# Column sums of the weights' squares: GpSimd's all-reduce over the partitions in the place of a TensorE product with ones

## The chip, the core and the metric

The kernel runs on one core of one Trainium2 chip. The metric is the device time of one execution in microseconds (us). Five engines matter here: TensorE (PE, with its weight loads listed as PEld), VectorE (DVE), ScalarE (ACT), GpSimd (POOL), and SyncE (SP), whose queue issues nearly all DMAs. Each engine runs its own list of instructions strictly in order; engines meet only at semaphores.

## What is computed

Three layers follow each other: an attention with normalised q and k, then two gated or rectified matrix layers. Cut to what matters:

```python
q_n, k_n = rmsnorm(q, g_q), rmsnorm(k, g_k)          # 4 batches, 12 heads, 448 x 64
scores = 1 / np.sqrt(64) * np.matmul(q_n, k_n.transpose(0, 1, 3, 2))
attn = softmax(scores)
x = np.matmul(attn, v)                               # -> 1792 tokens x 768
x = ((x @ w_a) * (x @ w_b)) @ w_out                  # 768 -> 1536 -> 768
h = x @ w_in                                         # 768 -> 2048
g = np.maximum(h, 0.0) + alpha * np.minimum(h, 0.0)
out = g @ w2_out                                     # 2048 -> 768
```

The inputs and weights reach the kernel as 64-bit floats.

## The kernel before

The matrix layers run as stages `a`, `y`, `h`, `o`, once for each of the 4 batches (`a0 y0 h0 o0 a1 ...`). A stage is cut into units: one unit is the weights of one 128-column block (or of a part of its rows), and 12 or 18 products of 128 x 128 by 128 x 448 on TensorE. A number is held as a sum of two 16-bit floats, so each block costs three products. The list `stream` holds the units of all stages in order: 24 units for `a`, 12 for `y`, 16 for `h`, 24 for `o`, then the same again for each batch.

The first time a unit's weights are used, four steps prepare them, each a fixed number of units ahead of the unit that TensorE works on (`STEPS`): `w_load` (10 ahead) reads the raw 64-bit weights, `w_convert` (8 ahead) makes 32-bit floats of them on ScalarE and VectorE and has ScalarE sum their squares along each partition (L659, into `ss`), `w_scale` (6 ahead) sums these over the 128 partitions and derives a power of two from the total, and `w_split` (3 ahead) splits the weights into two 16-bit halves with that scale (ScalarE L706, VectorE L707) and writes them to a scratch in HBM. Later batches only read the scratch. So all of this belongs to the 76 units of batch 0. Units share a scale in groups: two columns of two units in `a` and `h`, two parts of one column in `y`, four parts in `o`. That makes 12 + 6 + 8 + 6 = 32 sums over the partitions.

Such a sum is `total` (L125 to L135): a product of the squares with a matrix of ones on TensorE (tile `tot` from `ss` and `ones`; as the operands are 32-bit, the chip runs it as two passes), and for `y` and `o` a short VectorE sum over the parts (`tots`, L131). `power` (L110 to L121) then takes three short VectorE instructions: `pw` (L115), `sc` (L118), `inv_*` (L121). `total` also serves three other sums (of v, of the products a*b, of alpha), which stay as they are.

Attention is a second stream of work. It is emitted between the units (`RATE` says how many attention steps fall on a unit), and shares ScalarE (L435 exponential, L480 probabilities), VectorE (L418 maximum, L481 probabilities) and TensorE with the weight preparation. At the end of stage `o`, four small GpSimd instructions build the output scale `cum` (L893 to L896), and one more updates `icg` (L692).

The program's order on each engine isn't the order of the source: a scheduler places each instruction where it expects it to be ready, except those marked to be kept in program order.

Of the kernel before, what the change touches and what calls it, by code (L numbers as in the profile page):

```python
# [7 lines left out]

F32 = mybir.dt.float32
# [6 lines left out]
AX = mybir.AxisListType  # L16
# [3 lines left out]
def attention_gated_mlps_kernel(  # L20
# [15 lines left out]
    nc = tc.nc  # L36
# [21 lines left out]
    sm_p = ctx.enter_context(tc.tile_pool(name="sm", bufs=4))  # L58
# [48 lines left out]
    def mm(o, a, b, first, last):  # L107
        nc.tensor.matmul(out=o, lhsT=a, rhs=b, start=first, stop=last)  # L108

    def power(total, s, i):  # L110


        n = total.shape[1]
        h = sm_p.tile([128, 4], I32, tag="pw", name="pw")[:, 0:n]
        nc.vector.tensor_scalar(  # L115
            h, total.bitcast(I32), 1, 0x7F800000, op0=ALU.logical_shift_right, op1=ALU.bitwise_and
        )
        nc.vector.tensor_scalar(  # L118
            s.bitcast(I32), h, -1.0, float(205 << 23), op0=ALU.mult, op1=ALU.add
        )  # L120
        nc.vector.tensor_scalar(i.bitcast(I32), h, 1.0, float(49 << 23), op0=ALU.mult, op1=ALU.add)  # L121

    def total(cols, n, groups=1):

        ps = ps_x.tile([128, 512], F32, tag="x", name="tot")  # L125
        p = cols.shape[0]
        mm(ps[:, 0:n], ones[:p], cols, True, True)
        if n == groups:
            return ps[:, 0:n]
        t = sm_p.tile([128, 4], F32, tag="tot", name="tots")[:, 0:groups]  # L130
        nc.vector.reduce_sum(  # L131
            out=t, in_=ps[:, 0:n].rearrange("p (g k) -> p g k", g=groups), axis=AX.X
        )
        return t
# [476 lines left out]
    for st in stages:  # L611
        n, parts, _ = CHAINS[st[0]]
# [3 lines left out]
    def size(kind):  # L616
        return CHAINS[kind][2] * 128
# [17 lines left out]
    def w_convert(u):  # L635
        if u not in raws:
            return
        kind, n, part = stream[u]
        raw = raws.pop(u)
        pair = raw.bitcast(I32).rearrange("p (n t) -> p n t", t=2)  # L640
        lo, hi = pair[:, :, 0], pair[:, :, 1]
        t = wf_p.tile([128, 768], F32, tag="wf", name="wf")[:, 0:size(kind)]
        ti = t.bitcast(I32)

        nc.scalar.activation(  # L645
            out=t, in_=hi.bitcast(F32), func=AF.Prelu, scale=2.0 ** -112, alpha=-(2.0 ** 32)
        )
        i = nc.vector.tensor_scalar(ti, ti, 3, None, op0=ALU.logical_shift_left)
        if u == 0:
            tc.keep_in_program_order(i)  # L650
        nc.vector.scalar_tensor_tensor(  # L651
            out=ti, in0=lo, scalar=29, in1=ti, op0=ALU.logical_shift_right, op1=ALU.bitwise_or
        )
        wf[u] = t
        _, parts, _ = CHAINS[kind]
        j = (n * parts + part) % (parts * GROUP[kind])
        if j == 0:
            sums[0] = sm_p.tile([128, 4], F32, tag="ss", name="ss")
        nc.scalar.activation(  # L659
            out=junk(768, size(kind)), in_=t, func=AF.Square, accum_out=sums[0][:, j:j + 1]  # L660
        )
        if j == parts * GROUP[kind] - 1:
            squares[u] = sums[0][:, 0:j + 1]

    sums, squares = [None], {}

    def w_scale(u):

        if u not in squares:
            return  # L670
        kind, n, part = stream[u]
        _, parts, _ = CHAINS[kind]
        chains = GROUP[kind]
        us = range(u - parts * chains + 1, u + 1)
        sc = sm_p.tile([128, 2], F32, tag="sc", name="sc")[:, 0:chains]
        iv = inv[kind][:, n - chains + 1:n + 1]
        power(total(squares.pop(u), len(us), chains), sc, iv)
        for x in us:
            scales[x] = sc[:, (x - us[0]) // parts:(x - us[0]) // parts + 1]
        if (kind, n) == ("h", KF2 - 1):  # L680
            h_scales()

    def h_scales():

        mx = sm_p.tile([128, 1], F32, tag="mh", name="mh")
        ci = sm_p.tile([128, 1], F32, tag="mh", name="ci")
        nc.vector.tensor_reduce(out=mx, in_=inv["h"], axis=AX.X, op=ALU.max)
        nc.vector.tensor_scalar(
            ci.bitcast(I32), mx.bitcast(I32), -1.0, float(254 << 23), op0=ALU.mult, op1=ALU.add
        )  # L690
        nc.vector.tensor_scalar(cgf, inv["h"], ci, cg, op0=ALU.mult, op1=ALU.mult)
        nc.gpsimd.tensor_tensor(icg, icg, mx, op=ALU.mult)  # L692
        state["cgf"] = True
# [3 lines left out]
    def junk(width, n):  # L697
        return one_p.tile([128, width], BF16, tag="junk", name="junk")[:, 0:n]
# [13 lines left out]


    STEPS = [(w_load, 10), (w_convert, 8), (w_scale, 6), (w_split, 3)]
    AGAIN = [(w_load, 4)]
    cur = [0]
# [202 lines left out]
    if True:  # L919
# [37 lines left out]
        for i, st in enumerate(stages):  # L957
# [4 lines left out]
            n, parts, _ = CHAINS[s]  # L962
# [38 lines left out]
```

## Time and profile before

| what | value |
|---|---|
| three runs | 1245.96, 1240.85, 1245.94 us; median 1245.94 us |
| span of the profiled execution | 1240.7 us (its own time isn't given apart from the span; the nearest run is 1240.85 us) |
| PE busy | 1169.5 us (94%) |
| ACT busy | 740.8 us (60%) |
| DVE busy | 679.8 us (55%) |
| POOL busy | 9.2 us (1%) |
| sums over partitions for the scale | 32, all between 58.7 and 425.0 us |

The shares are averages over two very different stretches: up to about 430 us all engines prepare weights and run attention together; from about 560 us on TensorE's products follow one another. A busy share must be read from the stretch that the change touches.

### The profile page before, as it was taken

The numbers are of one execution on the slowest core, as the hardware profiler recorded it, in microseconds if no ns is written. First come the engines' busy times: TensorE is split into PE (matmuls) and PEld (weight loads), VectorE is DVE, ScalarE is ACT, GpSimd is POOL, SyncE is SP. The second block draws the span as 40 slices with busy tenths as digits, with TensorE's granted clock in tenths as the row PEclk, the third lists the DMA queues.
The fourth block names the chain that finished last, engine by engine and source line by source line (L and its number), as shares of the span: only waits on it lengthen the run. The fifth ranks groups of instructions, "written<-read, shape, count | busy, mean of one in ns | idle before, by whom it ended". The sixth has DMA issues, their size and how long they took to land.

```text
span 1240.7 us, 18165 instructions
## 1 busy us (share of the span) xinstructions
PE 1169.5 (94%) x6574; PEld 598.9 (48%) x6574; DVE 679.8 (55%) x1455; ACT 740.8 (60%) x1504; POOL 9.2 (1%) x32
## 2 busy tenths in 40 slices
PE   6897998889999799989999999999999999999998
PEld 3553554444444444434455454545555555555554
DVE  7988998979999766677651466332111440102400
ACT  6998999989999966677642465543311441213311
POOL 1000000000000000000000000000000000000000
PEclk9997999897999999999999999999999999999999
DMA  6546999999999999987953737876333333344343
GB/s 185 172 139 184 287 323 306 297 277 306 302 269 300 268 258 243 228 189 183 213 160 115 177 117 164 187 190 164 102 115 115 115 115 110 106 143 131 98 126 90
DMA packets 311242, 234.67 MB, mean 189 GB/s; under 512 B 175440, under 2 KB 284496, under 8 KB 311152
## 3 DMA queue, kind: packets, MB, share of 16 engines
q1 hardware_dynamic: 311040, 233.43, 71.2%
q8 instruction: 52, 0.85, 0.3%
q0 software_dynamic: 112, 0.07, 0.1%
q14 instruction: 38, 0.31, 0.1%
HBM read 155.79 MB, written 32.24 MB: 152 GB/s over the span
## 4 chain that ended last, share of the span: by engine, by line
PE 53%; ACT 1%; DMA 1%; DVE 0%; issue 0%; SPq 0%; ACTq 0%
PE p L108 48%; PE s L108 2%; PE x L108 2%; DMA pT<-p 1%; PE p L884 1%; ACT t L877 0%; ACT pf L435 0%; PE norm L108 0%; ACT p L480 0%; DVE nm L418 0%; SPq L487 0%; DVE p L481 0%; ACT x L531 0%; PE tot L108 0%; DVE v L387 0%
## 5 line engine op out<-in xcount | busy, mean ns | idle before, releaser
L108 PEld LDWEIGHTS <-w 128*128 128x128 f16 x4896 | 475.9, 99 | 473.3 <-issue 45.3
L108 PE MATMUL p<-x,w 128*128 128x448 f16 x1728 | 335.9, 353 | 2.8 <-ACT t L780 2.0
L108 PE MATMUL p<-g,w 128*128 128x448 f16 x1152 | 230.0, 356 | 5.8 <-ACT w L706 2.5
L108 PE MATMUL p<-y,w 128*128 128x448 f16 x1152 | 223.3, 355 | 0.0
L108 PE MATMUL p<-ab,w 128*128 128x448 f16 x864 | 169.6, 356 | 1.7 <-ACT ab L761 1.6
L418 DVE TENSOR_REDUCE nm<-s 128x2 f32<-128x896 f32 x84 | 91.0, 1085 | 38.0 <-PE s L108 37.6
L480 ACT ACTIVATE p<-pf,ri 128x448 f16<-128x448 f32 x126 | 81.8, 663 | 35.3 <-DMA pT<-p 27.6
L108 PE MATMUL s<-kT,qT 128*64 128x448 f16 (+1 forms) x336 | 89.2, 433 | 14.1 <-ACT pf L435 10.3
L481 DVE SCALAR_TENSOR_TENSOR p<-pf,ri,p 128x448 f16<-128x448 f32 x126 | 84.4, 681 | 32.9 <-ACT p L480 32.7
L435 ACT ACTIVATE pf<-s,nm,esc 128x448 f32<-128x448 f32 x126 | 90.0, 718 | 1.3
L859 DVE SCALAR_TENSOR_TENSOR t<-t,al,p 128x448 f32<-128x448 f32 x55 | 37.3, 678 | 95.0 <-ACT t L858 95.0
L783 DVE SCALAR_TENSOR_TENSOR ab<-p,inv_a,t 128x448 f32<-128x448 f32 x48 | 32.6, 678 | 95.5 <-PE p L108 95.4
L707 DVE SCALAR_TENSOR_TENSOR w<-wf,sc,w 128x768 f16<-128x768 f32 (+1 forms) x76 | 70.0, 928 | 5.6 <-ACT w L706 5.3
L877 ACT ACTIVATE t<-p,inv_o 128x448 f32<-128x448 f32 x24 | 25.5, 1063 | 77.3 <-PE p L108 77.3
L645 ACT ACTIVATE wf<-raw 128x768 f32<-128x768 f32 (+1 forms) x76 | 63.1, 831 | 13.0 <-DMA raw<-in_moe_w_in_dram 5.4
L786 ACT ACTIVATE junk<-ab 128x448 bf16<-128x448 f32 x48 | 27.4, 571 | 68.1 <-DVE ab L783 68.0
L651 DVE SCALAR_TENSOR_TENSOR wf<-raw,wf 128x768 int32<-128x768 int32 (+1 forms) x76 | 66.0, 869 | 0.4
L706 ACT ACTIVATE w<-wf,sc 128x768 f16<-128x768 f32 (+1 forms) x76 | 65.0, 863 | 0.7 <-issue 0.7
L659 ACT ACTIVATE junk<-wf 128x768 bf16<-128x768 f32 (+1 forms) x76 | 58.9, 775 | 4.1 <-DVE sc L118 1.2
L858 ACT ACTIVATE t<-p 128x448 f32<-128x448 f32 x55 | 29.8, 541 | 46.8 <-PE p L108 46.4
L844 ACT ACTIVATE g<-t,cgf 128x448 f16<-128x448 f32 x55 | 36.7, 668 | 34.6 <-DVE t L859 34.6
L845 DVE SCALAR_TENSOR_TENSOR g<-t,cgf,g 128x448 f16<-128x448 f32 x55 | 37.5, 682 | 29.5 <-ACT g L844 29.5
(139 smaller groups left out, 1029.1 us busy)
## 6 DMA issues: line engine op xcount, KB each, us to landing
w<-sc_a SPq DMA_DIRECT2D x72, 384.0 KB, 3.1
w<-sc_h SPq DMA_DIRECT2D x48, 384.0 KB, 3.0
w<-sc_o SPq DMA_DIRECT2D x72, 256.0 KB, 3.1
w<-sc_y SPq DMA_DIRECT2D x36, 384.0 KB, 3.1
raw<-in_moe_w_in_dram SPq DMA_DIRECT2D x16, 768.0 KB, 7.3
raw<-in_moe_w_out_dram SPq DMA_DIRECT2D x24, 512.0 KB, 5.5
raw<-in_moe_w_a_dram SPq DMA_DIRECT2D x12, 768.0 KB, 7.0
raw<-in_moe_w_b_dram SPq DMA_DIRECT2D x12, 768.0 KB, 6.5
```

The source lines that it names most:

```text
L108: nc.tensor.matmul(out=o, lhsT=a, rhs=b, start=first, stop=last)
L418: nc.vector.tensor_reduce(out=nm, in_=ps[:, :, 0:S], axis=AX.X, op=ALU.max, negate=True)
L435: nc.scalar.activation(out=pf, in_=ps[:, j, 0:S], func=AF.Exp, bias=nm[:, j:j + 1], scale=scale[j], accum_out=su[:, j:j + 1],)
L480: nc.scalar.activation(out=t[:, 0, :, 0:KP], in_=pf, func=AF.Copy, scale=r)
L481: nc.vector.scalar_tensor_tensor(out=t[:, 1, :, 0:KP], in0=pf, scalar=r, in1=t[:, 0, :, 0:KP], op0=ALU.mult, op1=ALU.subtract,)
L645: nc.scalar.activation(out=t, in_=hi.bitcast(F32), func=AF.Prelu, scale=2.0 ** -112, alpha=-(2.0 ** 32))
L651: nc.vector.scalar_tensor_tensor(out=ti, in0=lo, scalar=29, in1=ti, op0=ALU.logical_shift_right, op1=ALU.bitwise_or)
L659: nc.scalar.activation(out=junk(768, size(kind)), in_=t, func=AF.Square, accum_out=sums[0][:, j:j + 1])
L706: nc.scalar.activation(out=w[:, 0], in_=t, func=AF.Copy, scale=s)
L707: nc.vector.scalar_tensor_tensor(out=w[:, 1], in0=t, scalar=s, in1=w[:, 0], op0=ALU.mult, op1=ALU.subtract)
L845: nc.vector.scalar_tensor_tensor(out=x[:, 1], in0=t, scalar=cgf[:, f:f + 1], in1=x[:, 0], op0=ALU.mult, op1=ALU.subtract,)
L859: nc.vector.scalar_tensor_tensor(out=t, in0=t, scalar=al[:, f:f + 1], in1=ps, op0=ALU.mult, op1=ALU.add)
```

## The change

The sum over the partitions moves from `w_scale` to `w_convert`. As soon as the squares of a group's last unit are there, GpSimd's `partition_all_reduce` adds them over the 128 partitions, and every partition gets the total (`tw`). That is emitted 8 units ahead, `w_scale` stays 6 units ahead and passes `tw` to `power`; for `y` and `o` a VectorE sum over the parts stands in between as before.

```diff
+from concourse.bass_isa import ReduceOp
...
         if j == parts * GROUP[kind] - 1:
-            squares[u] = sums[0][:, 0:j + 1]
+            squares[u] = t = sm_p.tile([128, 4], F32, tag="tw", name="tw")[:, 0:j + 1]
+            nc.gpsimd.partition_all_reduce(t, sums[0][:, 0:j + 1], 128, ReduceOp.add)
...
-        power(total(squares.pop(u), len(us), chains), sc, iv)
+        t = squares.pop(u)
+        if parts > 1:
+            one = sm_p.tile([128, 1], F32, tag="tot", name="tots")
+            nc.vector.reduce_sum(out=one, in_=t, axis=AX.X)
+            t = one
+        power(t, sc, iv)
```

The built programs show how the orders move. On TensorE, in stage `a0`, the fourth sum stood between the products of two units. Before:

```order
L108 MATMUL p<-x_5_1462,w_1205 128x448
L108 MATMUL tot<-ss,ones 128x2 [waits PE_49]
L108 LDWEIGHTS w_1317
L108 MATMUL p<-x_0_559,w_1317 128x448
L108 LDWEIGHTS w_1317
```

With the change the products follow one another (lines are up to 7 higher behind the new code):

```order
L109 MATMUL p<-x_5_1464,w_1207 128x448
L109 LDWEIGHTS w_1319
L109 MATMUL p<-x_0_559,w_1319 128x448
```

On VectorE, the power step of the tenth sum (units 18 and 19 of `a0`) stood behind the split of two later weights and a maximum of attention. Before:

```order
L651 SCALAR_TENSOR_TENSOR wf<-raw,wf 128x768 [waits DMAHW5_49,DVE_49]
L707 SCALAR_TENSOR_TENSOR w_2104<-wf,sc,w_2104 128x768 [waits DMAHW1_49,Activation_49]
L707 SCALAR_TENSOR_TENSOR w_2141<-wf,sc,w_2141 128x768 [waits DMAHW4_49,PE_49,Activation_49]
L418 TENSOR_REDUCE nm<-s 128x2 [waits PE_49]
L648 TENSOR_SCALAR wf<-wf 128x768 [waits Activation_49]
L115 TENSOR_SCALAR pw<-tot 128x2 [waits PE_49]
```

With the change it stands directly behind the conversion, and waits for GpSimd:

```order
L652 SCALAR_TENSOR_TENSOR wf<-raw,wf 128x768 [waits DMAHW5_49,DVE_49]
L116 TENSOR_SCALAR pw<-tw 128x2 [waits Pool_49]
L354 TENSOR_TENSOR k_2239<-kr,k_2239 112x8x64
L119 TENSOR_SCALAR sc<-pw 128x2 [waits DVE_49]
L122 TENSOR_SCALAR inv_a<-pw 128x2
L419 TENSOR_REDUCE nm<-s 128x2 [waits PE_49]
```

On GpSimd, before, the first instructions of the output scale stood alone, from the end of `a0` to the end of stage `h0`:

```order
L893 TENSOR_TENSOR cum<-ix,iab 128x1 [waits DVE_49]
L894 TENSOR_TENSOR cum<-cum,iy 128x1 [waits DVE_49,Pool_49]
L692 TENSOR_TENSOR icg<-icg,mh 128x1 [waits DVE_49]
L895 TENSOR_TENSOR cum<-cum,icg 128x1 [waits Pool_49]
L896 TENSOR_TENSOR cum<-cum,ix 128x1 [waits Pool_49]
```

With the change the reductions stand between them, and an `ISA` row without operands, which loads another code library, wherever GpSimd goes from one kind to the other (eight in all):

```order
L665 ISA tw<-ss 128x2 [waits Activation_49] x11
L900 ISA
L900 TENSOR_TENSOR cum<-ix,iab 128x1 [waits DVE_49]
L665 ISA
L665 ISA tw<-ss 128x2 [waits Activation_49,Pool_49] x4
L665 ISA tw<-ss 128x2 [waits Activation_49]
L901 ISA
L901 TENSOR_TENSOR cum<-cum,iy 128x1 [waits DVE_49]
L665 ISA
L665 ISA tw<-ss 128x2 [waits Activation_49,Pool_49] x4
```

From stage `a1` on (about 430 us) TensorE's order is that of before.

## Rows read from the trace of the kernel before

**Rows 1.** The page, busy time and share of the span by engine

```profile
PE 1169.5 (94%) x6574; PEld 598.9 (48%) x6574; DVE 679.8 (55%) x1455; ACT 740.8 (60%) x1504; POOL 9.2 (1%) x32
```

**Rows 2.** Stretches: length, busy PE, PEld, DVE, ACT, POOL, PEclk, DMA share, GB/s

```profile
50.00:430.00 380.00, 340.25 (x1887) 173.72 (x1886) 338.51 (x741) 351.31 (x720) 1.66 (x5) 0.95 0.98 267
430.00:560.00 130.00, 122.02 (x736) 59.21 (x736) 88.77 (x191) 89.08 (x204) 0.12 (x1) 0.99 1.01 232
560.00:1241.00 681.00, 670.28 (x3712) 343.70 (x3708) 212.16 (x386) 260.59 (x494) 2.18 (x12) 1.00 0.52 138
```

**Rows 3.** Tile tot, whole span: count, ns least/median/most, first and last start

```profile
L108 PE MATMUL tot<-ss,ones x64: 167/251/374, 58.7 to 425.0; 128*128 128x2 f32 x52, 128*128 128x4 f32 x12
```

**Rows 4.** Timeline of PE near 130 us: start, us, engine, line, operation

```profile
130.00 0.28 PE L108 MATMUL tot<-ss,ones 128*128 128x2 f32 x2
130.14 3.19 PE L108 MATMUL p<-x,w 128*128 128x448 f16 x16
```

**Rows 5.** Waits of PE, 50 to 430 us: total us, times, longest

```profile
PE tot L108 <- ACT junk L659: 5.9, 4, 2.8
PE tot L108 <- DVE x L532: 4.9, 4, 2.1
```

**Rows 6.** Waits of ACT, 50 to 430 us

```profile
ACT wf L645 <- DMA raw<-in_moe_w_in_dram: 5.4, 6, 1.4
...
ACT nm L431 <- DVE nm L418: 2.9, 3, 2.0
...
ACT pT L463 <- PE x L108: 1.6, 2, 0.8
...
ACT wf L645 <- DVE w L707: 0.3, 1, 0.3
ACT y L821 <- PE p L108: 0.2, 1, 0.2
```

**Rows 7.** Waits of DVE, 50 to 430 us

```profile
DVE wf L648 <- ACT wf L645: 19.8, 20, 2.3
```

**Rows 8.** Timeline of POOL, its longest instruction and three of one shape

```profile
8.05 1.17 POOL L161 DMA_DIRECT2D al<-in_moe_alpha_dram  x1
...
286.77 0.44 POOL L894 TENSOR_TENSOR cum<-cum,iy 128x1 f32<-128x1 f32 x1 [63.72 <-DVE iy L121]
333.70 0.19 POOL L692 TENSOR_TENSOR icg<-icg,mh 128x1 f32<-128x1 f32 x1 [46.50 <-DVE mh L687]
...
334.24 0.64 POOL L896 TENSOR_TENSOR cum<-cum,ix 128x1 f32<-128x1 f32 x1
```

**Rows 9.** DMA issues: times, KB each, median us from issue to landing

```profile
sc_y<-w SPq DMA_DIRECT2D x12, 384.0 KB, 8.0
...
qS<-qT SPq DMA_DIRECT2D x36, 112.0 KB, 3.2
```

**Rows 10.** Timeline of ACT: last squares of sums 2, 10, 18 and 26 done

```profile
65.39 0.25 ACT L659 ACTIVATION_READ_ACCUMULATOR junk<-wf 128x1 f32 x1
...
172.03 0.18 ACT L659 ACTIVATION_READ_ACCUMULATOR junk<-wf 128x1 f32 x1
...
242.48 0.19 ACT L659 ACTIVATION_READ_ACCUMULATOR junk<-wf 128x1 f32 x1
...
325.15 0.21 ACT L659 ACTIVATION_READ_ACCUMULATOR junk<-wf 128x1 f32 x1
```

**Rows 11.** Timeline of DVE: what now stands ahead of power steps 2, 10, 18, 22, 26

```profile
65.41 0.45 DVE L450 TENSOR_SCALAR pf<-pf,ri 128x448 f32<-128x448 f32 x1
...
174.12 0.95 DVE L651 SCALAR_TENSOR_TENSOR wf<-raw,wf 128x768 int32<-128x768 int32 x1
...
247.70 0.68 DVE L481 SCALAR_TENSOR_TENSOR p<-pf,ri,p 128x448 f16<-128x448 f32 x1
...
293.40 0.56 DVE L648 TENSOR_SCALAR wf<-wf 128x768 int32<-128x768 int32 x1
...
326.22 1.02 DVE L707 SCALAR_TENSOR_TENSOR w<-wf,sc,w 128x768 f16<-128x768 f32 x1
```

## The prediction

> **What bounds the kernel now.** I read the page's busy shares first [rows 1]: TensorE stands at 94%, GpSimd at 1%. That seems to say that TensorE work is worth removing, and that GpSimd is free. The stretches say where [rows 2]. From 560 us on TensorE is busy 670.3 of 681 us, but no sum over partitions lies there: all 32 of them (64 records, two passes each) start between 58.7 and 425.0 us [rows 3], and the order of TensorE is the same in both programs from about 430 us on. So the change is decided between 50 and 430 us, and what is won or lost there shifts the rest. In these 380 us ScalarE is busy 351.3, TensorE 340.3 and VectorE 338.5 us. ScalarE is the fullest, at 92%, and the change takes nothing from it. The waits of ScalarE say what it lacks in its 28.7 idle us [rows 6]: five kinds of wait for TensorE, from the 1.6 us of the copy at L463 to the 0.2 us of L821, add up to 5.1 us (the others are 1.1 us each); nine kinds of wait for VectorE, from 2.9 to 0.3 us, add up to 8.6 us; most of what is left are waits for the raw weights, of which the largest kind is 5.4 us.
>
> **What is removed.** Thirty-two times two passes and their weight loads leave TensorE. What one costs is not its duration, since products are pipelined: at 130.00 us a sum starts, and the next product starts at 130.14 [rows 4]. So 32 x 0.14 = 4.5 us of TensorE's time go. Then the waiting: TensorE reached a sum before its input was there, and stood 5.9 us for ScalarE's squares and 4.9 us ahead of sums at which VectorE's x (L532) had come last [rows 5], 10.8 us in all. This is an upper bound, since some of these sums are those that stay. TensorE is relieved of up to 15.3 us. Of this ScalarE, the fullest engine, can get back what it now waits for TensorE, 5.1 us. I take **-5 us**, with 0 and -15.3 as ends.
>
> **What is added on GpSimd.** Thirty-two reductions of 128 x 2 or 128 x 4 numbers. The trace has no such instruction. The nearest rows from below are GpSimd's sums of two 128 x 1 tiles, 0.19 us at best [rows 8]. From above, something that carries data from some partitions to others without TensorE: the copy of q's halves by DMA, 3.2 us to landing [rows 9]. I take 1.2 us, after the longest instruction that GpSimd has in this trace, 1.17 us [rows 8], because a reduction over partitions is more than an elementwise sum and needs no descriptor's trip through memory. On GpSimd itself 32 x 1.2 = 38 us lie beside everything else. The Trainium skill (GPSIMD Engine Reference, Cross-partition) gives 247.7 us for GpSimd's partition reduction of 128 x 2048; an estimate from that figure is 0.24 us for two columns, by which the stalls below would be nothing; no run here shows it.
>
> **Where the wait goes.** TensorE no longer waits, VectorE does: its power step now waits for GpSimd, and all that is queued behind it on VectorE waits too (maxima of attention, splits, conversions), and through these ScalarE. The source says two units ahead, but the scheduler put the power step directly behind the place where it expected the sum, as the order of the tenth sum shows. So I read the lead that it has, on the clock of before: from the end of the last squares [rows 10] to the end of the VectorE instruction that now stands ahead of the power step [rows 11]. I take every eighth sum from the second. Sum 2: 65.86 - 65.64 = 0.2 us. Sum 10: 175.07 - 172.21 = 2.9 us. Sum 18: 248.38 - 242.67 = 5.7 us. Sum 26: 327.24 - 325.36 = 1.9 us. With a reduction of 1.2 us only sum 2 stalls, by 1.0 us; the mean is 0.25 us and 32 x 0.25 = 8 us of VectorE. With 0.19 us it is nothing. With 3.2 us the stalls are 3.0, 0.3, 0 and 1.3 us, a mean of 1.2, and 37 us in all. VectorE is idle 41.5 us in this stretch now, of which ScalarE loses the 8.6 us above, about a fifth. By the same share 8 us of stall cost ScalarE **+1.6 us**.
>
> **The library loads.** The order shows eight loads, where GpSimd goes between its output scale and its reductions. The one ahead of the first reduction and the last have idle time around them. Three round trips lie between reductions: at the ends of `a0`, `y0` and `h0`. In each, the way out is loaded while GpSimd waits for VectorE anyhow; the way back comes after. The tightest by my reading is `y0`: the output scale's instruction ends at 286.77 + 0.44 = 287.21 us [rows 8], then a load L and a reduction of 1.2 us follow, and power step 22 now stands behind an instruction that ended at 293.96 us [rows 11]. So 6.75 us are free, and L up to 5.55 us costs nothing. The trace has no load of another library; below, nothing excludes a load that takes next to no time, and a load cannot give time back. From above I take the slowest landing among the kernel's writes and loads, 8.0 us [rows 9], by which this place stalls 2.5 us and the three at most 7.4. I take **+1 us**. The Trainium skill (GPSIMD Engine Reference, Instruction dispatch) gives about 6 us, measured 5.95, for the first call of freshly loaded code, by which this place would stall 0.4 us; no run here shows it.
>
> **Small edits.** The power step and the sum of `y`'s and `o`'s parts now read a tile in SBUF instead of PSUM, with as many VectorE instructions as before: nothing. `tw` has four buffers, as many as the squares have: nothing. DMA issues don't change in number. The split keeps its place in ScalarE's order by a few rows: nothing either way that I can price.
>
> **The sum.** -5 + 1.6 + 1 = -2.4 us, against the span of 1240.7 us: 1238.3 us. The median of the runs lies 5.2 us above that span, so on the scale of the runs 1238.3 + 5.2 = 1243.5 us. That is 0.2% under the median of 1245.94 us, and a measurement of this kernel can tell about 0.5%, 6.2 us, from no change.
>
> **Rivals.**
>
> First, TensorE is what paces this stretch. It is only 11 us less busy than ScalarE there [rows 2], and a TensorE that stands delays attention's scores for all. Then the whole 15.3 us come back, with the stalls hidden in VectorE's idle time: 1240.7 - 15.3 + 5.2 = 1230.6 us. Against it: ScalarE waits for TensorE only 5.1 us [rows 6]. Chance 0.22.
>
> Second, **slower**: VectorE becomes the bound, at its power steps. It is busy 338.5 us and stands 19.8 us for ScalarE's conversion whatever happens [rows 2, 7], so 21.7 us of stall fit into the 380 us. By the four leads that is used up when a reduction takes about 2.5 us (stalls 2.3, 0, 0 and 0.6). At 3.2 us, 37 us of stall go over by 15 us; at 4 us the stalls are 3.8, 1.1, 0 and 2.1, 56 us in all, and go over by 34. In the middle, +25 us and none of TensorE's gain: 1240.7 + 25 + 1 + 5.2 = 1271.9 us. For it speaks a row: the same sum of two 128 x 1 tiles takes 0.19 us once, and 0.44 and 0.64 us elsewhere [rows 8], so something holds GpSimd up to 0.45 us. The Trainium skill (SBUF - State Buffer, Who interferes with whom) says that a VectorE instruction with two inputs in SBUF and a GpSimd instruction that reads SBUF exclude each other; the rows agree as far as they go, with 0.64 against 0.19 us, and by that rule each reduction could also hold VectorE for its own length, which would bring this case on at shorter reductions. Chance 0.22.
>
> Third, slower as well: the loads are long, since they come while the DMA engines are full (share 0.98 in this stretch [rows 2]). Each of the three round trips costs up to L - 5.55 us. From L = 7.6 us on that is more than 6 us; at L = 12 us it is 19 us and the time is about 1262 us. It needs more than the slowest landing shown. Chance 0.12.
>
> That the change doesn't do what it says is contained in the leads: the sum is two units ahead in the source, but not in VectorE's order.
>
> **How the numbers follow.** The forecast, 1243.5 us with its own range of 1236 to 1251, has a chance of 0.44; the rivals have 0.22, 0.22 and 0.12. The range that holds 8 in 10 leaves out the lower half of the first rival and the upper part of the second: 1231 to 1271 us. Faster than 1239.7 us are the first rival and the forecast's lower edge, 0.22 + 0.07 = 0.29; slower than 1252.2 us the second and third, 0.22 + 0.12 = 0.34; between, 0.37.
>
> **What would show it.** In the changed kernel's profile: no `tot<-ss` on TensorE, and ScalarE's waits for TensorE under 5 us between 50 and 430 us. GpSimd's reductions near 1.2 us; the waits of VectorE's power step and of the sum over parts for GpSimd near 8 us in all, most of them short. If these waits come to over 22 us and VectorE is full, the second rival holds. If three of them, behind the output scale's instructions, are several us each, it is the third. If ScalarE is fuller than 95% in a shorter stretch and `a1` begins over 10 us earlier, the first. The prediction is wrong at its root if VectorE's order in the leads doesn't tell when it really comes to the power step, since the clock of before is laid on another order.

## Result and profile after

The changed kernel takes 1250.01 us (median of six runs), the kernel before 1242.06 us beside it: 1.0064 times the time, 95% interval 1.0042 to 1.0086. It is 8 us slower, where the prediction had it 2.4 us faster.

The page of the changed kernel, and its stretches (columns as in [rows 2]):

```profile
PE 1169.0 (94%) x6510; PEld 593.0 (47%) x6510; DVE 679.3 (54%) x1455; ACT 740.6 (59%) x1504; POOL 33.0 (3%) x64
```

```profile
50.00:430.00 380.00, 338.69 (x1835) 167.08 (x1832) 339.38 (x738) 354.08 (x725) 24.92 (x36) 0.94 0.97 267
430.00:560.00 130.00, 119.41 (x711) 57.91 (x708) 82.62 (x176) 82.45 (x188) 0.00 (x0) 0.97 1.01 225
560.00:1241.00 681.00, 671.12 (x3702) 344.10 (x3703) 216.21 (x396) 261.65 (x500) 2.27 (x12) 0.99 0.53 138
```

Beside [rows 1, 2]: TensorE lost its 64 passes (6574 to 6510), GpSimd got 24 us of work, and from 50 to 430 us ScalarE did 2.8 us more work than before. By this reading the changed kernel is a little ahead there. From 430 to 560 us it did less on every engine (TensorE 119.4 against 122.0, ScalarE 82.5 against 89.1): there it fell behind.

The reductions, the waits of VectorE (50 to 434 us) and the larger waits of ScalarE for TensorE (50 to 430 us):

```profile
L665 POOL PARTITION_ALL_REDUCE tw<-ss x32: 398/481/1863, 45.2 to 422.4; - x32
```

```profile
DVE wf L649 <- ACT wf L646: 7.8, 10, 2.0
DVE tots L682 <- POOL tw L665: 6.6, 6, 3.2
...
DVE pw L116 <- POOL tw L665: 4.2, 11, 0.8
```

```profile
ACT x L532 <- PE x L109: 4.0, 2, 3.2
...
ACT pT L464 <- PE p L456: 2.1, 2, 1.7
ACT g L865 <- PE p L109: 1.9, 2, 1.1
ACT y L828 <- PE p L109: 1.5, 1, 1.5
...
ACT pT L464 <- PE x L109: 1.1, 2, 0.8
...
ACT t L787 <- PE p L109: 0.6, 1, 0.6
```

A reduction takes 0.48 us in the middle, not 1.2. VectorE stands 10.8 us for GpSimd, and 12.0 us less for ScalarE's conversion than in [rows 7]: by these sums the new waits lie where it stood before. But ScalarE's waits for TensorE, which were to vanish, are 12.0 us in all instead of 5.1 (the lines above, and three kinds of 0.3, 0.3 and 0.2 us).

Where the time goes is seen on TensorE at four places that both programs have. Timeline, first before, then after (the bracket: idle time, and what ended it):

```profile
221.00 0.60 PE L108 MATMUL tot<-ssab,ones 128*128 128x12 f32 x2 [2.76 <-ACT junk L786]
440.06 2.44 PE L108 MATMUL p<-g,w 128*128 128x448 f16 x12
557.43 0.39 PE L108 MATMUL tot<-ssab,ones 128*128 128x12 f32 x2 [3.18 <-ACT junk L786]
614.95 0.35 PE L108 MATMUL norm<-sq,onesb 128*128 128x448 bf16 x1 [1.41 <-ACT sq L822]
```

```profile
221.57 0.60 PE L109 MATMUL tot<-ssab,ones 128*128 128x12 f32 x2 [10.38 <-ACT junk L793]
436.30 2.44 PE L109 MATMUL p<-g,w 128*128 128x448 f16 x12
445.58 0.59 PE L109 MATMUL s<-kT,qT 128*64 128x448 f16 x2 [3.34 <-DMA kT<-k]
561.93 0.60 PE L109 MATMUL tot<-ssab,ones 128*128 128x12 f32 x2 [2.92 <-ACT junk L793]
621.49 0.35 PE L109 MATMUL norm<-sq,onesb 128*128 128x448 bf16 x1 [2.81 <-ACT sq L829]
```

At the end of stage `a0` TensorE needs the squares of all products a*b from ScalarE. It got there early and stood 10.4 us instead of 2.8: the gain is gone at 221 us. By 436 us the changed kernel is 3.8 us ahead again, at 562 us 4.5 behind, at 621 us 6.5 behind. These are single executions: four traces that have the sums and the order of before up to the second place (the kernel before, and `e2`, `x3` and `z1` below) reach it at 440.06, 437.21, 438.80 and 435.41 us, so a lead of 3.8 us there isn't clear of that spread. The last step is a transposed write of probabilities, and the 14 products after it (chain of waits, before and after):

```profile
609.67 3.35 DMA pT<-p
...
615.30 2.65 PE p L108 x14
```

```profile
614.78 4.77 DMA pT<-p
...
621.84 4.27 PE p L109 x14
```

The write lands 1.4 us later, TensorE stands longer, and the same products take 1.6 us more. Right after the longer idle time the granted clock is 0.83 in a stretch of 10 us, a mean between its two levels of 1.2 and 2.4 GHz, where the kernel before has 1.00 (length, busy PE, PEclk, DMA share, GB/s; two stretches before, then one after):

```profile
610.00:620.00 10.00, 8.59 (x49) 1.00 1.06 210
620.00:630.00 10.00, 10.00 (x55) 1.00 0.90 219
```

```profile
620.00:630.00 10.00, 8.51 (x40) 0.83 1.00 197
```

Behind that the shift stays at 8 us to the end.

### The profile page after: what moved, and what is told of

Its sections match the earlier page's. It is cut to its first block, busy times and chain, and to the rows that moved or that the text cites. A ratio compares the mean times of both kernels' runs of the same rounds, so it can differ in the third digit from the quotient of the medians.

```text
span 1248.9 us, 18080 instructions
## 1 busy us (share of the span) xinstructions
PE 1169.0 (94%) x6510; PEld 593.0 (47%) x6510; DVE 679.3 (54%) x1455; ACT 740.6 (59%) x1504; POOL 33.0 (3%) x64
## 4 chain that ended last, share of the span: by engine, by line
PE 52%; ACT 1%; DMA 1%; DVE 0%; issue 0%; SPq 0%; ACTq 0%
PE p L109 48%; PE s L109 2%; PE x L109 2%; DMA pT<-p 1%; PE p L891 1%; ACT t L884 0%; ACT pf L436 0%; PE norm L109 0%; ACT p L481 0%; SPq L488 0%; PE tot L109 0%; ACT junk L793 0%; DVE nm L419 0%; DVE p L482 0%; ACT x L532 0%
## 5 line engine op out<-in xcount | busy, mean ns | idle before, releaser
L109 PE MATMUL s<-kT,qT 128*64 128x448 f16 (+1 forms) x336 | 90.7, 433 | 21.8 <-ACT pf L436 15.3
```

## Experiments

Each engine's order can be pinned: `hold` adds dependencies without semaphores that chain an engine's instructions in a given order. "The order of before" below means that ScalarE, VectorE, TensorE and SyncE's queue are held to the order that the kernel before has. Ratios are against the kernel before on the same chip, with 95% intervals; a difference of two ratios carries the noise of both.

| kernel | ratio | interval |
|---|---|---|
| the change | 1.0064 | 1.0042 to 1.0086 |
| e1, order of before behind 434 us | 1.0061 | 1.0039 to 1.0082 |
| e2, TensorE's sums, the change's order behind 434 us | 1.0104 | 1.0074 to 1.0135 |
| e3, GpSimd's sums, order of before | 1.0054 | 1.0031 to 1.0078 |
| e4, change without library loads between sums | 1.0057 | 1.0036 to 1.0079 |
| l3, no sums at all, order of before | 1.0016 | 1.0001 to 1.0032 |
| l4, e3 without library loads | 1.0020 | 1.0005 to 1.0035 |
| x1, e1 without library loads | 1.0042 | 1.0030 to 1.0054 |

### Which part costs it

The first theory: the scheduler moved work of ScalarE, VectorE and SyncE's queue between 434 and 545 us, far from the sums, and that order is worse. The rival: GpSimd's sums with their waits and library loads. `e1` is the change with the old order behind 434 us, `e2` the kernel before with the new order there, `e3` the change in the order of before.

```diff
+    hold(nc, tc)   # e1, e2, e3: each with its own lists of orders
```

> The changed kernel, with every engine's order held: the changed kernel's order up to about 434 us, and behind it the order of before (which differs from the changed one only between about 434 and 545 us, on ScalarE, VectorE and SyncE's queue). Theory 1 (the loss comes from that later order, which the scheduler moved along): the 9 us lost there come back, 1238 to 1243 us, ratio to before 0.996 to 1.001. Theory 2 (GpSimd's sums, the waits for them and the library loads cost it): as the changed kernel, 1248 to 1252 us, ratio 1.005 to 1.008.

> The kernel before, sums on TensorE, with its own order held up to about 434 us and behind it the changed kernel's order on ScalarE, VectorE and SyncE's queue. No GpSimd reduction is in it. Theory 1: slower by what the changed kernel loses behind 434 us, 8 to 12 us, so 1250 to 1254 us, ratio 1.006 to 1.010. Theory 2: as before, 1242 us, ratio 0.998 to 1.002.

> The engine alone is swapped: sums by GpSimd as in the change, but TensorE (without the sums), ScalarE, VectorE and SyncE's queue all held to the order of before, so the power steps stand where they stood. Theory 1: 1237 to 1242 us, ratio 0.995 to 1.000, as TensorE is freed and VectorE hardly waits for GpSimd (under 3 us in all). Theory 2: the loads still cost, 1245 to 1250 us, ratio 1.003 to 1.007.

`e4` takes the library loads out instead: the five instructions of batch 0's output scale go to VectorE, so that GpSimd stays with its reductions.

```diff
-        nc.gpsimd.tensor_tensor(c, c, iy[:, b:b + 1], op=ALU.mult)
+        (nc.gpsimd if b else nc.vector).tensor_tensor(c, c, iy[:, b:b + 1], op=ALU.mult)
...
-        nc.gpsimd.tensor_tensor(icg, icg, mx, op=ALU.mult)
+        nc.vector.tensor_tensor(icg, icg, mx, op=ALU.mult)
```

> The changed kernel in its own order, but the five small instructions of batch 0's output scale on VectorE instead of GpSimd, so that no library load falls between the reductions. Theory 1: within 3 us of the changed kernel's 1250 us, since the three loads cost VectorE at most the 3 us that it waited at the end of stage a0. Theory 2, if the loads are the cost: back to 1242 to 1245 us.

Both causes are real: `e2` has no reduction and loses 1.0%, `e3` has the old order and loses 0.5%. But they don't add, and taking either away from the change (`e1`, `e4`) gave back nothing that can be told. In `e2` the new order shows where it hurts: the attention scores of `a1` wait 5.5 us for the transposed k (timeline of TensorE), where the kernel before has no such wait.

```profile
445.62 0.58 PE L108 MATMUL s<-kT,qT 128*64 128x448 f16 x2 [5.47 <-DMA kT<-k]
```

In `e3` one place tells of the library load: behind the output scale's instruction GpSimd's next reduction comes 10.55 us later, and VectorE stands 7.58 of them (timelines of GpSimd and VectorE). Behind the output scale's instruction of `a0` it is 5.96 us in the same trace; why this one is longer, the trace doesn't say.

```profile
283.69 0.67 POOL L901 TENSOR_TENSOR cum<-cum,iy 128x1 f32<-128x1 f32 x1 [7.75 <-ACT y L768]
294.91 0.41 POOL L665 PARTITION_ALL_REDUCE tw<-ss  x1 [10.55 <-issue]
```

```profile
295.35 0.17 DVE L116 TENSOR_SCALAR pw<-tw 128x2 int32<-128x2 int32 x1 [7.58 <-POOL tw L665]
```

### What paces the stretch

The prediction took ScalarE for the limit from 50 to 430 us. The rival is in the same rows: the DMA engines' share is 0.98 there [rows 2] (an approximate figure, since the next stretch has 1.01), and by the packet records of the trace they have packets in flight at every moment from 128 to 524 us. Six kernels in the order of before (`l1` to `l4`, `l6`, `l7`):

`l1`: half of the scratch writes left out.

```diff
-        nc.sync.dma_start(out=scratch[stream[u]], in_=w)
+        if stream[u][1] % 2 == 0:
+            nc.sync.dma_start(out=scratch[stream[u]], in_=w)
```

> The kernel before with its own order, but the scratch is written for even columns only, and the units of odd columns read an even column's scratch in the later batches (the same number of bytes is read). So 38 of the 76 scratch writes are left out (26 of 393 KB, 12 of 262 KB, 13.4 MB), and later batches compute with wrong weights for odd columns. Theory D: from 120 to about 480 us the DMA engines always have packets in flight, and the bytes pace the kernel, not ScalarE. The kernel before moves 91.0 MB in the 310 us from 120 to 430 us, 0.294 MB per us, so 13.4 MB are 45 us of it; ScalarE's 92% busy leaves up to 28 us to gain: ratio 0.964 to 0.985. Theory S (the prediction's): ScalarE paces this stretch, and no instruction of ScalarE is taken away: ratio 0.996 to 1.001.

Measured 0.9945 (0.9924 to 0.9966), 7 us less by this ratio and 9 by the medians. Neither held: ScalarE's theory gives nothing for fewer bytes, and the DMA theory expected 19 us or more.

`l2` is `l1` with GpSimd's sums.

> As the run with half of the scratch writes left out, but with the weights' sums on GpSimd; all other engines and queues are held to the order of the kernel before. To be read against that run, on the same chip. Theory D: with fewer bytes the engines pace more of this stretch, so taking 4.5 us of products and up to 10.8 us of waits off TensorE now shows: 3 to 10 us less than the same kernel with TensorE's sums (0.992 to 0.998 of it). Theory G (GpSimd's sums and library loads cost about 5 us whatever else bounds): 4 to 8 us more (1.003 to 1.007 of it).

Measured 0.9956 (0.9938 to 0.9974), 1234.02 against 1232.07 us: no gain from the freed TensorE here either. The loss is smaller than expected and, with both intervals, can't be told from nothing.

`l3`, without any sum over the partitions, is the one to remember:

```diff
-        power(total(squares.pop(u), len(us), chains), sc, iv)
+        squares.pop(u)
+        power(ones[:, 0:chains], sc, iv)
```

> The kernel before in its own order without the 32 sums over partitions (no products with ones, no sum over parts): the power step reads a constant 1 that is there from the start, so nothing waits for a sum; the scales are wrong. This is the most that any place for the sums can give. Theory S: the prediction's gain without its costs, 5 to 15 us: ratio 0.988 to 0.996. Theory D: the bytes pace, so little comes of it: 0.997 to 1.002.

Measured 1.0016 (1.0001 to 1.0032). All 32 sums and their waits gone, in the order of before, gives nothing. TensorE comes to the end of `a0` early and stands there:

```profile
219.13 0.60 PE L108 MATMUL tot<-ssab,ones 128*128 128x12 f32 x2 [6.74 <-ACT junk L787]
```

It stood 2.76 us before, so 4.0 us of the freed time are waiting again, and 1.9 us are left.

`l4` is `e3` with the edit of `e4`.

> GpSimd's sums with all else held to the order of the kernel before, but the five instructions of batch 0's output scale on VectorE, so that GpSimd loads no other library between its sums. The same without this last edit gave 1.0054. Theory G with the library loads as its cause: the stall near 290 us goes, ratio 0.998 to 1.002. If the loads matter little: 1.004 to 1.007 again.

Measured 1.0020 (1.0005 to 1.0035). In the order of before the library loads cost 0.34% (1.0054 to 1.0020), some 4 us and just clear of the noise of both, and the reductions themselves nothing that can be told beyond `l3`. `l2` has the loads too: there the gap that is 10.55 us in `e3` is 6.34 us, and VectorE stands 2.78 of it instead of 7.58.

`l6` drops ScalarE's 76 sums of squares too, `l7` in addition half of the scratch writes.

```diff
-        nc.scalar.activation(
-            out=junk(768, size(kind)), in_=t, func=AF.Square, accum_out=sums[0][:, j:j + 1]
-        )
```

> The kernel before in its own order without the sums over partitions and without the 76 sums of squares on ScalarE (0.83 + 0.19 us each, 78 us between 43 and 420 us); the scales come from a constant and are wrong. Theory S (ScalarE paces this stretch, as the prediction had it): the stretch shortens to the next fullest engine, TensorE with 340 of 380 us: 20 to 40 us less, ratio 0.968 to 0.984. Theory D (the DMA engines, always with packets in flight there, pace it): 0.993 to 1.002.

> As the run without sums and squares, and in addition without half of the scratch writes (which alone gave 0.9945, 9 us). Theory S: what it gives beyond the run without squares is small, within 3 us. Theory D: 0.985 to 0.995, that is 7 us or more beyond the run without squares. If two limits lie close together (DMA engines and ScalarE), both taken away give clearly more than the two gains together: over 20 us, ratio under 0.984.

`l6` measured 0.9966 (0.9953 to 0.9978). ScalarE is busy 688.8 us instead of 739.4 in `l3` (50.6 us less; the 78 us of the expectation added up rows that overlap). That much off the engine that was said to pace brings 4 us, 6 us against `l3`. In its trace `l6` is 9.9 us ahead of the kernel before at the place at 440 us and 4.2 us at the end, so more is won in the stretch than is kept. `l7` measured 0.9893 (0.9880 to 0.9906), 13 us, by the medians the 9 of `l1` and the 4 of `l6` together. In `l6` the freed ScalarE waits for its raw weights (page of `l3` and of `l6`, then stretch and waits of ScalarE of `l6`, 50 to 430 us):

```profile
PE 1164.1 (94%) x6510; PEld 591.6 (48%) x6510; DVE 678.7 (55%) x1443; ACT 739.4 (59%) x1504; POOL 9.5 (1%) x32
```

```profile
PE 1164.4 (94%) x6510; PEld 591.4 (48%) x6510; DVE 676.3 (55%) x1443; ACT 688.8 (56%) x1352; POOL 9.1 (1%) x32
```

```profile
50.00:430.00 380.00, 340.90 (x1878) 169.57 (x1875) 340.59 (x740) 307.82 (x586) 1.65 (x5) 0.95 0.97 271
```

```profile
ACT wf L645 <- DMA raw<-in_moe_w_out_dram: 11.9, 13, 2.4
ACT wf L645 <- DMA raw<-in_moe_w_in_dram: 7.9, 7, 2.3
...
ACT wf L645 <- DMA raw<-in_moe_w_b_dram: 6.4, 4, 2.6
```

ScalarE is 81% busy, and these waits are 26.2 us; in the kernel before the same three were 5.4 [rows 6], 4.5 and 1.8 us. The DMA engines stay at 0.97. But ScalarE's waits for TensorE grow as well, from 5.1 us before to 16.7. So ScalarE alone does not pace: freed, it runs into the weights' transfers and into TensorE. The DMA engines are not the only limit either: transfers that were estimated at 45 us brought 7 to 9 when taken away. What sets the rest isn't settled.

### Both causes together, and the later order

`x1` is `e1` with the edit of `e4`: both suspects gone.

> The change with both suspects taken away together: batch 0's output scale on VectorE (no library load between the sums), and from 434 us on the order of the kernel before on ScalarE, VectorE and SyncE's queue; up to 434 us the change's own order. Taken away one at a time, each left the loss as it was (1.0057 and 1.0061). Theory E (each of the two is enough alone, since what is gained up to 434 us is given back there whichever stands): 1.000 to 1.003. Theory O (a third cause, the change's order up to 434 us): 1.004 to 1.007 again.

Measured 1.0042 (1.0030 to 1.0054), at the lower edge of the second theory. Against `e1` the loads are worth 0.19%, against `e4` the later order 0.15%, each with about 0.25% of noise to both sides, so neither is clear of nothing. 0.42% stay, 0.22% more than `l4`, which differs by the order up to 434 us alone; that is just clear of its noise. In the change's own order TensorE stands 9.5 us at the end of `a0`, in `l4` 6.95.

`x3` splits the later order: ScalarE and VectorE as the change has them, SyncE's queue as before.

> TensorE's sums and the order of before up to 434 us; behind it ScalarE and VectorE in the order that the change brought, but SyncE's queue of DMAs in the order of before. With the queue in the new order too it was 1.0104. Theory Q (the queue's new order costs it, by loads that stand behind others): 0.998 to 1.003. Theory V (the order on ScalarE and VectorE): 1.007 to 1.012.

Measured 1.0128 (1.0110 to 1.0145): the order on ScalarE and VectorE suffices. ScalarE there comes to a probability whose transposed write isn't there (timeline of ScalarE):

```profile
508.44 0.67 ACT L480 ACTIVATE p<-pf,ri 128x448 f16<-128x448 f32 x1 [9.14 <-DMA pT<-p]
```

The queue alone in the new order wasn't tried. Part of these 9 us may come from the mixture, since the two orders belong together.

The traces show the cost of the later order more steadily than the totals do. From the second of the four places above to the third it is 117.4 us in the kernel before. In the five traces with the change's later order (the change, `e2`, `e4`, `x3`, `y3`) it is 123.7 to 130.7 us, in all fourteen with the order of before there 114.2 to 121.1. Why `e1`, with 119.2 us in this stretch against 125.6 in the change, is no faster as a whole isn't settled.

### The place at 610 us

At 557 us `l3` is 1.7 us ahead of the kernel before and `l4` level with it (the same sum of squares as above, at 555.69 and 557.31 us); from 620 us on both are some 2 us behind. The transposed write takes 4.72 us in `l3`. The packet records of the trace show what comes with it: each of `l3`, `l4`, `e3` and the change has one 16 KB packet of the instruction queue inside that write (at 610.5, 612.5, 617.2 and 616.2 us). The kernel before has its packets at 601.3 and 623.4 us. They come once per about 128 products, 52 in all:

```profile
q8 instruction: 52, 0.85, 0.3%
```

The sums taken off TensorE are 64 products and 64 weight loads, half of such a period: all later fetches move. The write's length follows the packets in all traces whose chain of waits goes through it: with such a packet inside, it takes 4.6 to 5.0 us (these four, `e4`, `l2`, `l6` and `l7`), without one 3.3 to 3.4 (the kernel before, `e2`, `l1`, `x3`, and `y1` to `y4` below). The slower products don't follow from it alone: in `e3`, `e4`, `l4` and `l7` the write is as long, and the 14 products take 2.65 us. To move the fetches back, 64 products that nobody reads were put ahead of TensorE's first:

```diff
         nc.vector.memset(onesb, 1.0)
+        pad = ps_x.tile([128, 512], F32, tag="x", name="pad")
+        for _ in range(64):
+            mm(pad[:, 0:2], onesb, onesb[:, 0:2], True, True)
```

`y1`, `y2`, `y3` and `y4` are `l4`, `l3`, the change and `x1` with this, `z1` is the kernel before with it.

> GpSimd's sums, no library load between them, all else in the order of before (1.0020), and 64 idle products ahead of TensorE's first. Theory F (TensorE's instruction fetch, moved by half a period, falls into the transposed write near 610 us): the fetch stands near 600 and 622 us again, that write lands in 3.3 to 3.7 us, and 2 to 4 us come back: ratio 0.998 to 1.000. Theory N (the fetch is chance company): 1.001 to 1.003 again.

> No sums over partitions, order of before (1.0016), and 64 idle products ahead of TensorE's first. Theory F: 2 to 4 us come back: ratio 0.997 to 0.9995, which would also be the most that taking the sums off TensorE can give. Theory N: 1.000 to 1.003 again.

> The change in its own order (1.0064), and 64 idle products ahead of TensorE's first. Theory F: of its 8 us the 3 to 4 us between 607 and 625 us come back: ratio 1.003 to 1.005. Theory N: 1.0055 to 1.0075.

> The change in its own order up to 434 us and in the order of before behind it, no library load between the sums (1.0042), and 64 idle products ahead of TensorE's first. Theory F: nothing is left of the loss, 0.999 to 1.002. Theory N: 1.003 to 1.0055 again.

> The kernel before in its own order, with nothing but 64 idle products ahead of TensorE's first, which move its instruction fetches by half a period, near 610 us. Theory F: the transposed write there lands in 4.5 to 5 us, and the kernel is 2 to 4 us slower: ratio 1.0012 to 1.003. Theory N (the place of the fetch costs nothing that can be measured): 0.999 to 1.001.

| kernel | without padding | with it | interval |
|---|---|---|---|
| l4, y1 | 1.0020 | 1.0009 | 0.9988 to 1.0030 |
| l3, y2 | 1.0016 | 1.0002 | 0.9983 to 1.0022 |
| change, y3 | 1.0064 | 1.0098 | 1.0062 to 1.0135 |
| x1, y4 | 1.0042 | 1.0014 | 0.9992 to 1.0035 |
| before, z1 | 1 | 0.9987 | 0.9967 to 1.0007 |

In the profiled executions the fetch does what was said: in `y1` to `y4` the write lands in 3.35 to 3.40 us and the 14 products take 2.65 us. Chain of waits, `l3` and then `y2`:

```profile
608.48 4.72 DMA pT<-p
...
615.48 4.32 PE p L108 x14
```

```profile
605.55 3.35 DMA pT<-p
...
611.17 2.65 PE p L108 x14
```

That is 3.0 us at this place. In the ratios it is less for `l4` and `l3` (1.4 and 1.7 us, within the noise) and 3.5 us for `x1`, just clear of it. `y1` lies between the two theories, `y2` in the range of N, `y4` in that of F, `y3` outside both. `z1` missed: its packet came at 605.1 us, 0.25 us ahead of the write, which landed in 3.85 us, and it got no slower. In `y3` the profiled execution took 1244.65 us and the five others 1251 to 1256; no trace shows where these lose, and its rise stays unexplained. What is shown is that the write is longer in a profiled execution when the fetch falls inside it; that this accounts for 3 of the change's 8 us in the median isn't.

## Why the prediction was wrong

**What bounds the kernel: failed, and with it the forecast.** "ScalarE is the fullest, at 92%" was read as "ScalarE paces". [rows 2] had a fuller column, the DMA share of 0.98, which came up only under the third rival. With 51 us taken off ScalarE the time fell by 4 us (`l6`), where the theory that it paces expected 20 or more. Freed, it stood for the weights' transfers and for TensorE instead. So 5 us of its waits were worth little from the start.

**What is removed, -5 us: nothing.** The counts were right (64 passes are gone), the price of the waits was not. Without any sum, and with nothing in its place, the time is 1.0016. The step took waits of ScalarE for TensorE as time that comes back. It did not ask what TensorE waits for next: the squares of `a0`, where it now stands 6.7 us (`l3`) or 10.4 us (the change) instead of 2.8. In the change ScalarE's waits for TensorE rose to 12.0 us. The first rival, which gave back all 15.3 us, falls with it.

**The reductions and VectorE's stalls: right in total by luck.** 0.48 us instead of 1.2, 10.8 us of waiting instead of 8. With 0.48 us only sum 2 stalls by the four leads, 0.3 us, or some 2 us for all 32; there were 17 waits, most of them short. The caveat holds: the leads, read on the clock of before, don't tell when VectorE comes there. In the order of before the reductions cost nothing that can be told (`l4` against `l3`). The second rival is out: VectorE is no fuller (339.4 against 338.5 us), and its 10.8 us are balanced by 12.0 us less of waiting for ScalarE.

**The library loads, +1 us: mechanism right, size open.** In the order of before they cost some 4 us (`e3` against `l4`). In the change's own order taking them out gave 0.9 us (`e4`) and 2.4 us (`x1` against `e1`), both within the noise. At `y0`, where up to 5.55 us were to cost nothing, the changed kernel's gap is 6.04 us and VectorE's power step doesn't wait. The longest stall is at the end of `a0` (timelines of GpSimd and VectorE):

```profile
230.26 3.02 POOL L900 TENSOR_TENSOR cum<-ix,iab 128x1 f32<-128x1 f32 x1 [9.32 <-DVE ab L769]
239.22 0.41 POOL L665 PARTITION_ALL_REDUCE tw<-ss  x1 [5.93 <-ACT w L713]
...
289.95 0.57 POOL L665 PARTITION_ALL_REDUCE tw<-ss  x1 [6.04 <-ACT p L481]
```

```profile
239.66 0.15 DVE L682 TENSOR_REDUCE tots<-tw 128x1 f32<-128x2 f32 x1 [3.16 <-POOL tw L665]
```

This is the place of the third rival, with loads of about 6 us instead of 12. The Trainium skill (GPSIMD Engine Reference, Instruction dispatch) gives 5.95 us for the first call of freshly loaded code; the gaps of 5.93 and 6.04 us agree, the 10.55 us in `e3` don't.

**"The order of TensorE is the same in both programs from about 430 us on": the place that was left out.** That is true. It was read as "what is won or lost there shifts the rest". But ScalarE, VectorE and SyncE's queue were in another order until 545 us, 100 us and more behind the last sum. That order costs 1.0% by itself (`e2`), and in the change's trace the stretch from 436 to 562 us is 8.3 us longer than before.

**The sum.** The forecast of 1243.5 us adds 5.2 us for the difference between the runs and the profiled span, from three runs; over six runs of the kernel before it is 1.4 us, so the forecast stands for 1239.7 us beside the 1242.06. The measured 1250.0 us lies in the forecast's own range of 1236 to 1251 us by luck, on the slower side and from causes that its sum doesn't have.

From `l4`, which has the reductions without their loads and nothing else of the change, to the change the ladder is: 2.5 us that `l4` loses (the kernel without sums loses 2.0 of them), 2.7 us for the order up to 434 us (`x1`, 1.0042 against 1.0020), and 2.7 us for loads and later order together (1.0064 against 1.0042), 7.9 us in all. The last two seem to overlap: with the other one gone, the loads read 2.4 us and the later order 1.9. The intervals are 1.5 to 2.7 us to each side, so the ladder's single steps are rough. With the idle products ahead, which are meant to change nothing but the place of the fetches, the steps come out otherwise: the order up to 434 us costs 0.6 us (`y4` against `y1`), loads and later order together 10.4 us (`y3` against `y4`), and only this is clear of the noise, though `y3`'s rise is itself unexplained. So it is shown that the sums' place had nothing to give, that the later order costs time by itself, and that the loads do in the order of before; how the change's 8 us divide among them stays open. What costs the 2.0 us without sums isn't settled either; the fetch at 610 us has that size in the traces.

## What to carry to other kernels

Work that is taken off a busy engine is worth what the kernel gains when the work is dropped altogether; that costs one run, and here it said "nothing", which would have settled the question of the best place. Before waits are booked as gains, ask what the relieved engine waits for next, and look at the DMA share beside the engines' busy shares. Where a scheduler orders the program, compare the orders of all engines and queues as far as they differ, not only around the edit.

## What the runs showed of the hardware

GpSimd's sum of two 128 x 1 tiles took 3.02 us at 230.26 us, against 0.19 us at best [rows 8]; VectorE was running instructions with two inputs in SBUF back to back then (timeline of VectorE):

```profile
225.54 7.23 DVE L769 SCALAR_TENSOR_TENSOR ab<-ab,sab,ab 128x448 f16<-128x448 f32 x12
```

The reductions spread from 0.40 to 1.86 us (3.45 in `e3`). The rule of the Trainium skill that the prediction cites (SBUF - State Buffer, Who interferes with whom) agrees with these rows as far as they go; the reverse, VectorE held for the length of a reduction, no run shows by itself.

Removing instructions moved the packets of the instruction queue here: 64 products fewer or more moved them past a transposed write or into it. One 16 KB packet inside that write went with 1.3 to 1.7 us of longer landing in eight traces. In four of these (the change, `l2`, `l3`, `l6`) a granted clock under 1.00 followed, and 14 products took 4.2 to 4.3 us instead of 2.65; in the four others they took 2.65 us after much the same idle time (2.87 us in `l4`, 2.81 us in the change).
